# Another element order for the first chunk of activations in a linear-attention plus feed-forward kernel

## The chip, the cores and the metric

The kernel runs on one core of a Trainium2 chip. Its engines are TensorE (PE: matmuls; PEld: loads of the stationary operand, which overlap PE), VectorE (DVE), ScalarE (ACT), GpSimd (POOL) and SyncE (SP, which here only issues DMAs). Each engine works through its own queue in order; where one needs another's result it waits on a semaphore. The metric is the time of one execution on the device in microseconds, the median of several; lower is better.

## What is computed

Two stages follow each other. The first is a linear attention over 8 batches of 8 heads, 576 tokens and 64 dimensions; the second is a feed-forward layer over the 4608 tokens of 512 features.

```
q_s = exp(q - max(q, -1));  q_s = q_s / (sum(q_s, -1) + 1e-9)      # over the head's 64 dimensions
k_s = exp(k - max(k, 2));   k_s = k_s / (sum(k_s, 2) + 1e-9)       # over the 576 tokens
kv  = einsum('bhsd,bhse->bhde', k_s, v)
x   = einsum('bhsd,bhde->bhse', q_s, kv)  as [4608, 512]           # tokens x (heads * 64)
h   = x @ w_in                                                      # [4608, 2048]
g   = h * 1 / (1 + exp(-beta * h))
out = g @ w_out                                                     # [4608, 512]
```

All inputs and the output are f32 in DRAM; the large matmuls run in bf16.

## The kernel before

**Chunks and units.** The feed-forward layer works on x transposed: features on the 128 partitions, in four k tiles (kt 0 to 3), 512 tokens along the free axis. A *chunk* is 512 tokens. Chunks 0 to 6 are the first 512 tokens of the batches 0 to 6, chunk 7 holds the last 64 tokens of all eight batches, chunk 8 is batch 7. A *unit* is one chunk with 128 of the 2048 hidden features, so there are 16 units for each chunk, numbered through: 0 to 15 are chunk 0. A unit n goes through three steps, named in the plan `h_n`, `th_n`, `g_n` and `o_n`: four matmuls, one for each k tile, add up x times w_in in a PSUM bank (`st1`, line 863, matmul at 879); ACT takes the tanh (line 897) and DVE gates with it (line 914); four matmuls multiply by w_out into the accumulators (line 945).

**The order.** A plan written out by hand (`ORDER`) lists all steps, and each engine's queue gets its instructions in this order. `uses` and `made` in the code only check that the plan does not run ahead of itself. The waits between engines are put in by the framework that builds the program, from what each instruction reads and writes of a tile.

**Chunk 0.** PE has nothing to do for the feed-forward layer until x of batch 0 is there; until then it runs filler matmuls (line 367, on a constant or on the exponentials `eqe`) between the attention's own. So that it can begin early, chunk 0 is cut in two halves of 256 tokens, h = 0 and 1 (`cols(h)`), for the units 0 to 3. Two such units share a PSUM bank for each half. In the plan `h_n_h_x` stands for unit n, half h and the k tiles x and x + 2; whole units are `h_n`.

**x of batch 0.** x leaves PE in four PSUM banks, one for each half h and each member jp of a pair of heads (`x_mm`, line 688, written `x_0_h_J`). A bank holds, for both J = 0 and 1, 256 tokens of k tile 2J + jp. Four evacuations, `xev_0_h_jp` in the plan, cast them from f32 to bf16 into the tile `xT[0]` (`x_ev_half`, line 714; it calls `cast`, whose instruction has line 232 on ACT and 234 on DVE). `xT[0]` is laid out as [k tile, 512 tokens], so one evacuation writes two pieces of 256 elements: one in k tile jp and one in k tile 2 + jp. Within a piece the tokens are written in an order with a step of two elements.

The part of the plan around it:

```
xev_0_0_0=dve, qrcp_0_2, x_0_1_1, qnorm_0_2_0=pool,
qnorm_0_2_1=pool, xev_0_0_1=act, x_0_1_0, fill_10, fill_5, cast_w2_0=pool, ld_w2_1, xev_0_1_0=dve, ld_w1_0, ld_w1_1,
cast_w2_1=pool, h_0_0_0, h_0_0_1, h_1_0_0, h_1_0_1, h_0_1_0, xev_0_1_1=act, th_0_0, th_1_0, h_0_1_1, qmax_1_2,
h_1_1_0, h_1_1_1, ld_w4_0, g_0_0, ld_w4_1, qmax_1_3, h_2_0_0, h_2_1_0, ld_k1_0, th_0_1, th_1_1, g_0_1, qsub_1_1=pool,
```

Behind these come the halves of the units 2 and 3, then `h_6`, `h_4`, `h_5`, `h_7` as whole units and `o_0_1`, the first step with w_out. The weights are loaded in f32 and cast to bf16 in blocks: `cast_w0` (first block of w_in, units 0 to 3), `cast_w2` (second block of w_in, units 4 to 7), `cast_w1` and `cast_w3` (first and second block of w_out).

**Later use of the tile.** `xT` has two buffers; `xT[0]` is written again for chunk 2 (`x_ev`, line 707), which like all other chunks writes one k tile of 512 tokens at a time, in the layout [k tile, 512 tokens].

Of the kernel before, what the change touches and what calls it, by code (L numbers as in the profile page):

```python
# [117 lines left out]
def kernel(  # L118
# [40 lines left out]
    def sbt(name, shape, dt):  # L159
        return sb.tile(shape, dt, name=name)  # L160
# [30 lines left out]
    xT = [sbt(f"xT{i}", [P, KT, 512], BF16) for i in range(2)]  # L191
# [14 lines left out]
    def take(*who):  # L206
        assert sum(last in done for last, _ in turns) >= len(who), who
        for w in who:
            n = next(n for n, (last, _) in enumerate(turns) if last in done)
            i = turns.pop(n)[1]  # L210
            place[w] = ring[i][:]
            turns.append((w, i))

    def made(what, *parts):
        done.update((what, p) for p in parts)

    def uses(what, *parts):
        for p in parts:
            assert (what, p) in done, (what, p)
# [10 lines left out]
    def cast(eng, dst, src):  # L230
        if eng is act:
            act.copy(dst, src)  # L232
        else:
            eng.tensor_copy(dst, src)  # L234
# [57 lines left out]
    for b in range(B):  # L292
        n = 2 if b else 1
# [26 lines left out]
    def cast_w(n, half, eng, c0=0, c1=512):  # L320
        which, blk = W[n]
        s = wst[n % 4][:, 2 * half : 2 * half + 2, c0:c1]
        if which == "i":
            made("i", *[(4 * blk + c // P, half) for c in range(c0, c1, P)])
            cast(eng, w_in_b[:, 2 * half : 2 * half + 2, 512 * blk + c0 : 512 * blk + c1], s)
        else:
            made("o", 2 * blk + half)
            cast(eng, w_out_b[:, 4 * blk + 2 * half : 4 * blk + 2 * half + 2, :], s)

    for n in range(8):  # L330
        for half in range(2):
            op(f"ld w{n} {half}", lambda n=n, half=half: load_w(n, half))
            if n == 0:
                for c, (c0, c1) in enumerate(((0, P), (P, 512))):
                    op(
                        f"cast w{n} {half} {c}",
                        lambda e, n=n, half=half, c0=c0, c1=c1: cast_w(n, half, e, c0, c1),
# [361 lines left out]
    def mixed(x):  # L699
        return x.rearrange("p (t c i) -> p t i c", i=2, c=64)  # L700
# [6 lines left out]
    def x_ev(b, j, eng):  # L707
# [3 lines left out]
        done.add(("x", b, j))  # L711
        cast(eng, mixed(xT[b % 2][:, j, :]), place[("x", b, j)].rearrange("p (t i c) -> p t i c", i=2, c=64))

    def x_ev_half(b, jp, h, eng):
        uses("xmm", (b, 0, h), (b, 1, h))
        made("xT", (b, jp, h), (b, 2 + jp, h))
        x = xT[b % 2][:].rearrange("p (J c) (t n i) -> p c J t i n", c=2, i=2, n=64)
        w = place[("x", b, jp, h)].rearrange("p (J t i n) -> p J t i n", J=2, t=2, i=2)
        cast(eng, x[:, jp, :, 2 * h : 2 * h + 2], w)

    def xt_mm(b):
        uses("kvn", *pairs_of(b, 0, 2))
# [55 lines left out]
    for h in range(3):  # L778
        i0, i1 = 4 * h, min(4 * h + 4, NI)
        for J in range(2):  # L780
            p = dict(j=2 * J, n=2, i0=i0, i1=i1)
            op(f"qmax 0 {h} {J}", lambda p=p: q_max(0, **p))
            if (h, J) in QPE:
                op(f"qin 0 {h} {J}", lambda h=h, J=J: q_in(h, J))
                op(f"qminus 0 {h} {J}", lambda h=h, J=J: q_minus(h, J))
            else:
                op(f"qsub 0 {h} {J}", lambda e, p=p: q_sub(0, eng=e, **p), "pool")
            op(f"qexp 0 {h} {J}", lambda p=p: q_exp(0, **p))
            op(f"qsum 0 {h} {J}", lambda p=p: q_sum(0, **p))
            if h < 2:  # L790
                op(f"qrcp 0 {h} {J}", lambda p=p: q_rcp(0, **p))
            op(f"qnorm 0 {h} {J}", lambda e, J=J, i0=i0, i1=i1: q_norm(0, 2 * J, 2, e, i0, i1), "pool")
            if h < 2:
                op(f"qtr 0 {h} {J}", lambda J=J, h=h: q_tr(0, J, 4 * h, 4))
                op(f"qtrev 0 {h} {J}", lambda e, J=J, h=h: q_tr_ev(0, J, 4 * h, 4, e), "act")
                op(f"x 0 {h} {J}", lambda J=J, h=h: x_mm(0, J, h))
                op(f"xev 0 {h} {J}", lambda e, J=J, h=h: x_ev_half(0, J, h, e), "dve" if J else "act")
            else:
                op(f"qtrtev 0 {J}", lambda e, J=J: q_tr_ev(0, J, NM, 1, e), "act")
        if h == 2:  # L800
            op(f"qrcp 0 {h}", lambda i0=i0, i1=i1: q_rcp(0, 0, KT, i0, i1))
# [37 lines left out]
    def chunk_x(c):  # L839
        if c == TAILS:  # L840
            return xTt
        return xT[(c if c < TAILS else c - 1) % 2]

    def halves(h):
        return (0, 1) if h is None else (h,)

    def cols(h):
        return slice(0, 512) if h is None else slice(256 * h, 256 * h + 256)
# [3 lines left out]
    def bank(n, h):  # L852
        key = ("h", n) if h is None else ("hp", n // 2, h)
        if key not in place:
            take(key)
        if h is None:
            return place[key]
        return place[key][:, 256 * (n % 2) : 256 * (n % 2) + 256]
# [4 lines left out]
    def st1(n, ks=(0, 1, 2, 3), h=None):  # L863
        c, u = divmod(n, NJ)
        x = chunk_x(c)
        for kt in ks:
            uses("i", (u, kt // 2))
            if c == TAILS:
                uses("xTt", *[(b, kt % 2) for b in range(B)])
            else:  # L870
                uses("xT", *[(c - (c > TAILS), kt, a) for a in halves(h)])
        if h is not None and n % 2 and ks[0] == 0:
            uses("st1", (n - 1, h))
        if ks[0]:
            uses("begun", (n, h))
        made("begun", (n, h))
        w = bank(n, h)
        for kt in ks:
            pe.matmul(  # L879
                w,  # L880
                w_in_b[:, kt, u * P : (u + 1) * P],
                x[:, kt, cols(h)],
                start=(kt == 0),
                stop=(kt == KT - 1),
            )
        if KT - 1 in ks:
            made("st1", *[(n, a) for a in halves(h)])
# [93 lines left out]
    for n in range(NU):  # L981
        if n < LEAD:
            for h in range(2):
                for x in range(2):
                    op(f"h {n} {h} {x}", lambda n=n, h=h, x=x: st1(n, (x, x + 2), h))
                op(f"th {n} {h}", lambda n=n, h=h: tanh(n, h))
                if n % 2 == 0:
                    op(f"g {n} {h}", lambda n=n, h=h: gate(n, h))
                op(f"o {n} {h}", lambda n=n, h=h: st2(n, h))
            continue  # L990
        if n in (16, 17):
            op(f"h {n} 0", lambda n=n: st1(n, (0, 1)))
            op(f"h {n} 1", lambda n=n: st1(n, (2, 3)))
        else:
            op(f"h {n}", lambda n=n: st1(n))
        op(f"th {n}", lambda n=n: tanh(n))
        op(f"g {n}", lambda n=n: gate(n))
        if n >= NU - LAST:
            for t in range(3):
                op(f"o {n} {t}", lambda n=n, t=t: st2(n, ts=[t]))  # L1000
            for x in range(2):
                op(f"o {n} 3 {x}", lambda n=n, x=x: st2(n, ts=[3], xs=[x]))
        else:
            op(f"o {n}", lambda n=n: st2(n))
# [12 lines left out]
    with tc.manual_schedule():  # L1017
        for name, _, e in plan:
            fn, eng = ops[name]
            eng = e or eng  # L1020
# [31 lines left out]
```

## Time and profile before

| | |
|---|---|
| median of 3 runs | 288.67 us (288.48 to 288.77) |
| the profiled execution | 288.57 us |
| its span, first to last instruction | 286.8 us |
| granted TensorE clock over the span | 0.999 |
| PE, share of the span busy | 96% |
| DVE | 68% |
| ACT | 61% |
| POOL | 46% |

Times in the rows are microseconds from the start of the span, unless they are called ns. A row in order of time begins with the start and the length of one or several merged instructions, then engine, line, operation, what it writes and reads, and their number; in brackets stands for how long the engine was idle before it, and what ended that. `xT<-acc` are the evacuations of batch 0, `xT<-hT` those of the later batches, since these go through the banks called hT. Matmuls are pipelined: the length of one is longer than the distance to the next.

### The profile page before, as it was taken

To read this page: it belongs to the slowest core of one execution; us is meant where nothing else is said; L and a number is where in the kernel's file an instruction comes from. 1 tells how busy PE (TensorE), PEld (TensorE's weight loads), DVE (VectorE), ACT (ScalarE), POOL (GpSimd) and SP (SyncE) were. 2 spreads that over 40 slices of the span, in tenths; PEclk is the share of its full clock that TensorE was granted. 3 is DMA by queue.
4 is the path that set the end of the run, shared out by engine and by line. 5 is a ranking of instruction groups with operands and counts; after the bars stand their busy time and mean duration, and the time that the engine had idled before them with its cause. 6 is when DMAs were issued, how large, how long until landed. Compare 5 with 4: busy or idle time off the path is not lost.

```text
span 286.8 us, 5158 instructions
## 1 busy us (share of the span) xinstructions
PE 276.6 (96%) x1947; PEld 130.0 (45%) x1977; DVE 194.7 (68%) x393; ACT 174.3 (61%) x291; POOL 131.2 (46%) x93
## 2 busy tenths in 40 slices
PE   7798999999999999999999999999999999999994
PEld 3355544444444544444444444444444444444442
DVE  2996966999899898987667948555754254435420
ACT  2488885887498567846587556564672274345422
POOL 6897896959469958082970561090020000000000
PEclk9999999999999999999999999999999999999999
DMA  7999999990891994991533907000054001004204
GB/s 225 396 388 387 384 390 391 369 346 4 225 385 50 292 278 192 299 325 61 165 119 98 235 29 192 0 3 2 0 123 181 0 0 39 0 0 180 78 1 146
DMA packets 36905, 50.01 MB, mean 174 GB/s; under 512 B 15745, under 2 KB 16017, under 8 KB 36881
## 3 DMA queue, kind: packets, MB, share of 16 engines
q1 hardware_dynamic: 36736, 49.56, 52.9%
q8 instruction: 15, 0.25, 0.3%
q10 hardware_dynamic: 144, 0.13, 0.1%
q14 instruction: 10, 0.07, 0.1%
HBM read 36.71 MB, written 9.44 MB: 161 GB/s over the span
## 4 chain that ended last, share of the span: by engine, by line
PE 91%; DVE 3%; DMA 2%; ACT 2%; issue 1%; SPq 0%; DVEq 0%
PE hT L879 43%; PE acc L945 42%; DMA qf<-in_q_dram 2%; PE hT L638 2%; PE hT L688 1%; DVE km L490 1%; DVE qs L428 1%; PE hT L937 1%; PE acc L937 1%; DVE qm L378 1%; ACT ek L612 0%; SPq L275 0%; ACT w_in_b L232 0%; PE hT L464 0%; DVE xT L234 0%
## 5 line engine op out<-in xcount | busy, mean ns | idle before, releaser
L897 ACT ACTIVATE th<-hT,beta_c 128x512 bf16<-128x512 f32 (+1 forms) x148 | 96.6, 676 | 66.7 <-PE hT L879 47.3
L914 DVE SCALAR_TENSOR_TENSOR g<-th,hT 128x512 bf16<-128x512 bf16 x144 | 94.7, 680 | 60.4 <-ACT th L897 57.2
L945 PE MATMUL acc<-w_out_b,g 128*128 128x512 bf16 x543 | 130.7, 380 | 1.4 <-issue 0.8
L879 PE MATMUL hT<-xT,w_in_b 128*128 128x512 bf16 (+1 forms) x517 | 118.0, 373 | 1.9 <-ACT xT L232 0.8
L879 PEld LDWEIGHTS <-w_in_b 128*128 128x128 bf16 x592 | 57.5, 98 | 66.5 <-issue 1.0
L945 PEld LDWEIGHTS <-g 128*128 128x128 bf16 x560 | 53.7, 98 | 64.5 <-issue 2.9
L560 POOL TENSOR_TENSOR kf<-kf,kmb 128x1152 f32<-128x1152 f32 (+1 forms) x15 | 38.0, 2546 | 23.6 <-DVE kmb L550 17.7
L441 POOL TENSOR_TENSOR qn<-eqe,qz 128x1152 bf16<-128x1152 bf16 (+2 forms) x20 | 34.5, 1738 | 28.1 <-DVE qz L433 18.1
L393 POOL TENSOR_TENSOR qf<-qf,qm 128x1152 f32<-128x1152 f32 (+2 forms) x20 | 34.4, 1734 | 19.4 <-issue 14.5
L378 DVE TENSOR_REDUCE qm<-qf 128x9 f32<-128x576 f32 (+2 forms) x34 | 23.3, 703 | 5.9 <-DMA qf<-in_q_dram 5.9
L422 ACT ACTIVATE eqe<-qf 128x576 bf16<-128x576 f32 (+2 forms) x34 | 21.5, 657 | 9.3 <-POOL qf L393 9.3
L232 ACT CAST xT<-hT 128x512 bf16<-128x512 f32 x19 | 12.5, 739 | 21.1 <-PE hT L688 21.1
L428 DVE TENSOR_REDUCE qs<-eqe 128x9 f32<-128x585 bf16 (+2 forms) x34 | 24.0, 713 | 0.5 <-ACT eqe L422 0.4
L490 DVE TRANSPOSE_TENSOR_REDUCE km<-kf 128x18 f32<-128x576 f32 x32 | 23.6, 754 | 0.0
L612 ACT ACTIVATE ek<-kf 128x576 bf16<-128x576 f32 x30 | 19.5, 682 | 0.9 <-POOL kf L560 0.9
L234 POOL CAST va<-vf 128x1152 bf16<-128x1152 f32 (+1 forms) x11 | 12.0, 1104 | 7.0 <-DMA vf<-in_v_dram 7.0
L879 PE MATMUL hT<-xTt,w_in_b 128*128 128x512 bf16 x63 | 14.9, 380 | 0.1
L234 DVE CAST xT<-hT 128x512 bf16<-128x512 f32 x9 | 6.3, 727 | 7.0 <-PE hT L688 7.0
L232 ACT COPY osb<-acc 128x512 f32<-128x512 f32 x14 | 7.8, 594 | 3.0 <-PE acc L945 3.0
L367 PE MATMUL hT<-g,warm 128*128 128x512 bf16 x21 | 7.7, 520 | 1.6 <-POOL g L240 1.5
L234 DVE COPY osb<-acc 128x512 f32<-128x512 f32 (+1 forms) x6 | 3.8, 632 | 4.9 <-PE acc L937 3.8
L638 PEld LDWEIGHTS <-ek 64*64 64x64 bf16 x576 | 5.7, 106 | 2.2 <-issue 1.3
(73 smaller groups left out, 121.8 us busy)
## 6 DMA issues: line engine op xcount, KB each, us to landing
qf<-in_q_dram SPq DMA_DIRECT2D x14, 576.0 KB, 6.2
kf<-in_k_dram SPq DMA_DIRECT2D x14, 576.0 KB, 7.9
vf<-in_v_dram SPq DMA_DIRECT2D x14, 576.0 KB, 7.3
out_dram<-osb SPq DMA_DIRECT2D x19, 256.0 KB, 2.6
wst<-in_moe_w_in_dram SPq DMA_DIRECT2D x8, 512.0 KB, 8.3
wst<-in_moe_w_out_dram SPq DMA_DIRECT2D x8, 512.0 KB, 10.2
out_dram<-wst SPq DMA_DIRECT2D x16, 256.0 KB, 3.7
qf<-in_q_dram SPq DMA_DIRECT2D x4, 288.0 KB, 4.0
```

Source lines behind the costliest of these rows:

```text
L234: eng.tensor_copy(dst, src)
L378: dve.tensor_reduce(qm[:, j : j + n, i0:i1], qf[b % 2][:, j : j + n, i0:i1], axis=AX.X, op=ALU.max,)
L393: eng.tensor_tensor(x, x, m, ALU.subtract)
L422: act.activation(eq[:, i0:i1, j : j + n, :].rearrange("p i j d -> p j i d"), x, ACTF.Exp)
L428: dve.tensor_reduce(qs[:, i0:i1, j : j + n].unsqueeze(3), x, axis=AX.X, op=ALU.add)
L441: eng.tensor_tensor(qn[b % 2][:, i0:i1, j : j + n, :], eq[:, i0:i1, j : j + n, :], z, ALU.mult)
L490: dve.tensor_reduce(km[:, j : j + n].rearrange("p j i e -> p (j i e)"), kf[b % 2][:, j : j + n].rearrange("p j i (e c) -> p (j i e) c", c=32),
L560: eng.tensor_tensor(x, x, m, ALU.subtract)
L879: pe.matmul(w, w_in_b[:, kt, u * P : (u + 1) * P], x[:, kt, cols(h)], start=(kt == 0), stop=(kt == KT - 1),)
L897: act.activation(th[turn(n, h) % 3][:, c], bank(n, h), ACTF.Tanh, scale=beta_c[:, u : u + 1])
L914: dve.scalar_tensor_tensor(out=out, in0=of, scalar=1.0, in1=src, op0=ALU.add, op1=ALU.mult)
L945: pe.matmul(acc[t][:], g[n % NG][:, t * P : (t + 1) * P], w_out_b[:, u, :], start=(u == 0), stop=(u == NJ - 1),)
```

## The change

`xT[0]` gets a second view, `x_first`, which orders its 2048 elements as [half h, member j, J, 256 tokens] instead of [k tile, 512 tokens]. The evacuations of batch 0 write through this view, and all units of chunk 0 read through it. An evacuation thus writes 512 adjacent elements. A half unit reads 256 adjacent elements for each k tile, as before but elsewhere in the tile. A whole unit (4 to 15) reads two pieces of 256 elements, 1024 elements apart, where it read 512 adjacent ones; its PSUM bank is written through a view of two halves, which are adjacent. The plan is not touched, and the later chunks keep the old layout, also in `xT[0]`.

```diff
+    x_first = xT[0][:].rearrange("p k t -> p (k t)").rearrange("p (h j J c) -> p j J h c", h=2, j=2, J=2)
+
     def x_ev_half(b, jp, h, eng):
         uses("xmm", (b, 0, h), (b, 1, h))
         made("xT", (b, jp, h), (b, 2 + jp, h))
-        x = xT[b % 2][:].rearrange("p (J c) (t n i) -> p c J t i n", c=2, i=2, n=64)
+        x = x_first[:, jp, :, h].rearrange("p J (t n i) -> p J t i n", i=2, n=64)
         w = place[("x", b, jp, h)].rearrange("p (J t i n) -> p J t i n", J=2, t=2, i=2)
-        cast(eng, x[:, jp, :, 2 * h : 2 * h + 2], w)
+        cast(eng, x, w)
...
         w = bank(n, h)
+        if c == 0 and h is None:
+            w = w.rearrange("p (h c) -> p h c", h=2)
         for kt in ks:
+            r = x[:, kt, cols(h)]
+            if c == 0:
+                r = x_first[:, kt % 2, kt // 2]
+                r = r if h is None else r[:, h]
             pe.matmul(
                 w,
                 w_in_b[:, kt, u * P : (u + 1) * P],
-                x[:, kt, cols(h)],
+                r,
                 start=(kt == 0),
                 stop=(kt == KT - 1),
             )
```

## The prediction

> **What bounds the kernel now.** I read the page first, then the waits of the stretch from 19 to 23 us, then the order of time from 8 to 31 us, and last the stage sums up to 66 us.
>
> ```profile
> span 286.8 us, 5158 instructions
> PE 276.6 (96%) x1947; PEld 130.0 (45%) x1977; DVE 194.7 (68%) x393; ACT 174.3 (61%) x291; POOL 131.2 (46%) x93
> PE 91%; DVE 3%; DMA 2%; ACT 2%; issue 1%; SPq 0%; DVEq 0%
> 22.90:66.00 43.10, 42.77 (x293) 21.10 (x297) 36.19 (x74) 34.67 (x59) 33.98 (x23) 1.00 0.99 365
> 66.00:276.00 210.00, 208.22 (x1458) 96.18 (x1481) 140.94 (x278) 123.83 (x203) 78.34 (x38) 1.00 0.41 121
> ```
>
> TensorE is the bound: 96% busy, 91% of the chain that ended last. In the two stage rows the first number after the length is PE's busy time: from 22.9 us on it idles for 0.33 us of 43.10 and for 1.78 us of 210. So PE's time can only be won ahead of 22.9 us, where first the attention of batch 0 must be done, and there the change lies. These are all the waits above 0.3 us of that place (who waited for whom, us in total, times, longest):
>
> ```profile
> ACT xT L232 <- PE hT L879: 1.7, 1, 1.7
> PE hT L879 <- ACT xT L232: 0.8, 1, 0.8
> PE hT L879 <- DVE xT L234: 0.4, 1, 0.4
> ```
>
> And the same in order of time (start, length, engine, line, operation):
>
> ```profile
> 19.43 0.41 PE L688 MATMUL acc<-qT,kvn 64*64 64x256 bf16 x8
> 19.48 0.74 DVE L234 CAST xT<-acc 128x512 bf16<-128x512 f32 x1 [0.22 <-ACT beta_c L349]
> 19.62 0.77 ACT L232 CAST xT<-acc 128x512 bf16<-128x512 f32 x1
> 20.18 0.70 DVE L234 CAST xT<-acc 128x512 bf16<-128x512 f32 x1
> 20.27 0.27 PE L879 MATMUL hT<-xT,w_in_b 128*128 128x256 bf16 x1
> 20.94 1.16 PE L879 MATMUL hT<-xT,w_in_b 128*128 128x256 bf16 x9 [0.40 <-DVE xT L234]
> ...
> 22.14 0.73 ACT L232 CAST xT<-acc 128x512 bf16<-128x512 f32 x1 [1.75 <-PE hT L879]
> 22.73 0.83 ACT L897 ACTIVATE th<-hT,beta_c 128x256 bf16<-128x256 f32 x2
> 22.91 6.02 PE L879 MATMUL hT<-xT,w_in_b 128*128 128x256 bf16 x38 [0.81 <-ACT xT L232]
> ```
>
> The four CASTs are the evacuations xev_0_h_J, in the order (half 0, member 0) on DVE, (0, 1) on ACT, (1, 0) on DVE, (1, 1) on ACT. The first ten matmuls are h_0_0_0, h_0_0_1, h_1_0_0, h_1_0_1, h_0_1_0. Two waits are odd. The second matmul reads kt 2 of half 0, written by the first evacuation like kt 0, which began at 20.27; yet it starts at 20.94, after the third evacuation (20.18 + 0.70 = 20.88), which writes half 1. And the last evacuation, whose input was ready at 19.43 + 0.41 = 19.84 and whose engine was free at 20.39, waits 1.75 us until the tenth matmul has read its data, though nothing before it reads what it writes.
>
> One reading explains both. In xT[0] (k tile times 512 + token) an evacuation writes two pieces of 256, 1024 apart; as one interval from its first to its last element, (0,0) covers 0 to 1280, (0,1) 512 to 1792, (1,0) 256 to 1536 and (1,1) 768 to 2048. The second matmul reads 1024 to 1280, inside (1,0); the first reads 0 to 256, outside it. The fifth pair, h_0_1_0, reads 1280 to 1536 with its second matmul, inside (1,1), and that is the one the ACT cast waits for. So the waits are those of interval against interval. Two evacuations whose intervals meet ran at once (19.48 and 19.62), so two-piece write against two-piece write is told apart; only a single-piece read against a two-piece write is not.
>
> **The change part by part.** In the new order of xT[0] (half, member, J, 256 tokens) evacuation (h, j) writes 512 adjacent elements from h*1024 + j*512, and the reads of the units 0 to 3 are single pieces of 256 inside them. No instruction is added, removed or put elsewhere in any queue, no DMA is touched, no wait is added.
>
> *The evacuations themselves.* Same 512 elements, same inner order and same step of two elements. Those of batch 1, which already write one piece each, give the price:
>
> ```profile
> L232 ACT CAST xT<-hT 128x512 bf16<-128x512 f32 x19 | 12.5, 739 | 21.1 <-PE hT L688 21.1
> L234 DVE CAST xT<-hT 128x512 bf16<-128x512 f32 x9 | 6.3, 727 | 7.0 <-PE hT L688 7.0
> ```
>
> 739 and 727 ns stand against 0.70 to 0.77 us above: I take no difference, bounds -0.04 to +0.04 us for the one that could matter.
>
> *The false wait of the second matmul.* Nine matmuls take 1.16 us with one length of 0.27 us in it, so they are issued every (1.16 - 0.27) / 8 = 0.111 us. Without the wait the second starts at 20.27 + 0.11 = 20.38. The third reads what ACT ends at 19.62 + 0.77 = 20.39 and has its turn at 20.49, 0.1 us later: no wait. The ninth (half 1, member 0) has its turn at 20.27 + 8 x 0.111 = 21.16, and DVE ends at 20.88: none either.
>
> *The false wait of the last evacuation.* ACT starts it when it is free, at about 20.43, and ends at 20.43 + 0.74 = 21.17. The eleventh matmul, which now starts at 22.91, has its turn at 20.27 + 10 x 0.111 = 21.38: 0.2 us to spare, and this is the next thing that would be late. Gain of PE here: 22.91 - 21.38 = **1.53 us**. At the least the two idle times go, 0.40 + 0.81 = 1.21; the rest is the length of matmuls that had to end, not only be issued, before ACT could go.
>
> *Does it stay won?* The 38 matmuls from 22.91 run without a break, so what feeds them must come 1.53 us sooner. tanh of the first pair waits for matmul eight: 20.27 + 7 x 0.111 + 0.27 = 21.32 instead of 22.73, 1.41 sooner. What hangs on it:
>
> ```profile
> 21.46 2.02 POOL L234 CAST w_in_b<-wst 128x1024 bf16<-128x1024 f32 x2
> ...
> 23.59 0.69 DVE L914 SCALAR_TENSOR_TENSOR g<-th,hT 128x512 bf16<-128x512 bf16 x1 [2.08 <-ACT th L897]
> 24.20 0.75 DVE L378 TENSOR_REDUCE qm<-qf 128x9 f32<-128x576 f32 x1
> ...
> 25.03 2.12 POOL L393 TENSOR_TENSOR qf<-qf,qm 128x1152 f32<-128x1152 f32 x1 [1.55 <-DVE qm L378]
> ```
>
> DVE waited 2.08 us for that tanh, POOL 1.55 us for the DVE reduction behind the gate; so DVE and POOL move 1.4 us with it, and the later tanhs, which wait for PE, the full 1.53. The first whole unit, h_6, comes after 22 half matmuls: 22.91 + 22 x 0.111 = 25.35 now, 23.82 then. Its weights are POOL's two casts, done at 21.46 + 2.02 = 23.48 and not moved: 0.3 us to spare. Its bank is freed by the gate at 23.59 + 0.69 - 1.4 = 22.9.
>
> What cannot come sooner is the data from DRAM, for the DMA share up to 66 us is 0.99. The load with the least time between landing and use that I found is the second half of w_out's second block:
>
> ```profile
> L318 SPq DMA_DIRECT2D wst<-in_moe_w_out_dram x1: 688/688/688, 25.5 to 25.5; - x1
> DMA to landing us min/median/max: 11.1/11.1/11.1
> 38.56 1.06 ACT L232 CAST w_out_b<-wst 128x1024 bf16<-128x1024 f32 x1
> ```
>
> It lands at 25.5 + 11.1 = 36.6 and is cast at 38.56: 1.96 us, above 1.53. So I let the whole gain stand until the end.
>
> *The whole units 4 to 15 of chunk 0* (12 x 4 = 48 matmuls) read two pieces of 256, 1024 apart. No matmul of the trace has just that; the nearest are the fillers that read eqe in pieces of 64 (two at a time), beside those that read one piece:
>
> ```profile
> 7.81 0.81 PE L367 MATMUL hT<-g,warm 128*128 128x512 bf16 x3
> 9.82 0.38 PE L367 MATMUL hT<-g,warm 128*128 128x512 bf16 x1
> 10.47 1.02 PE L580 MATMUL acc<-kf,ident_f 128*128 128x512 f32 x2
> 13.38 0.59 PE L367 MATMUL hT<-eqe,warm 128*128 128x512 bf16 x2
> ```
>
> One piece: (0.81 - 0.38) / 2 = 0.215 us each. Eight pieces: 0.59 - 0.38 = 0.21. So two pieces cost nothing; as the rows are rounded to 0.01 us, the bounds are -0.005 to +0.005 us each, 48 of them -0.25 to +0.25 us. The costliest 512 columns of the trace are the f32 ones, 1.02 / 2 = 0.51 us each; that end is 48 x (0.51 - 0.215) = 14 us, and I keep it for a rival.
>
> By the Trainium skill (Advanced Engine Details and Errata, SBUF Cachelines) accesses that stay in a 16-byte line run at full performance; 256 bf16 values fill 32 such lines, so by it too these reads would cost nothing, as the fillers' rows say.
>
> *The sum.* The profiled execution took 288.57 us, 1.77 us of it outside the span of 286.8. 288.57 - 1.53 = 287.04. The median of the runs is 0.10 above that execution, so **287.1 us**.
>
> **The rivals.** *Half of it.* If only ACT's false wait goes, the tenth matmul starts at 20.94 + 8 x 0.111 = 21.83 as now and the eleventh at 21.94: gain 0.97, 287.7. If only the matmul's goes, ACT waits until 20.27 + 9 x 0.111 + 0.27 = 21.54, ends about 22.3 and PE resumes at about 22.35: gain 0.56, 288.1. For it: one of the two waits may have another cause. Against: one reading fits both, to the matmul. A part of the gain lost at one of the spare times above (0.2, 0.3, 0.4 us) ends in the same region. Chance 0.12.
>
> *The change does not do what it says*: the waits stay, as the written element order still has a step of two. Against it speaks chunk 1, whose evacuations write one piece with that step:
>
> ```profile
> 49.30 1.93 ACT L232 CAST xT<-hT 128x512 bf16<-128x512 f32 x3 [3.12 <-PE hT L688]
> 50.25 3.62 PE L879 MATMUL hT<-xT,w_in_b 128*128 128x512 bf16 x16
> ```
>
> PE reads the finished k tiles from 50.25 while ACT writes the others until 51.23. Time 288.7. Chance 0.06.
>
> *The other side: the split read is slow.* Each of the 48 matmuls would pay for its second piece, PE having nothing to hide it behind. It cancels the gain at 1.53 / 48 = 0.032 us each; to lose 0.2% takes 0.044. At the rate of the f32 row, +14 us, it would be 301. Against it stand the eqe fillers. The Trainium skill (Advanced Engine Details and Errata, PSUM Cachelines) says that any non-contiguous access pattern "significantly slows down matmuls"; here the output is only viewed as two halves and stays adjacent in its bank, so by its words the rule would not bite, and no run here shows it. Chance 0.06.
>
> **How the numbers follow.** The forecast has 0.76. I call 0.2%, 0.58 us, what a measurement of this kernel can tell from no change. The forecast's own range is 287.1 with +-0.25 for the reads and 0.1 for evacuations and run-to-run, 286.75 to 287.45; the range reaches to 288.1 to take in the halved gains and to 286.7 below; the unchanged and the slow-read case are left out. Faster: 0.76 and nearly all of the 0.12, 0.86. The same: 0.06 and a little of both neighbours, 0.08. Slower: 0.06.
>
> **What would show it.** In the changed profile the first ten matmuls of the unit line stand in one row with the rest, from about 20.3 us, with no idle time put down to a cast; the fourth evacuation starts near 20.4 on ACT; PE resumes the eleventh matmul near 21.4; its tanh starts near 21.3 and the unbroken run that now ends at 22.91 + 6.02 = 28.93 ends near 27.4. The matmuls of the whole units of chunk 0 still follow each other every 0.215 us. Wrong it would be if PE shows new idle time between 22 and 66 us, at h_6 or behind a landing, that eats the 1.5 us, or if those matmuls come more slowly.

## The result and the profile after

The changed kernel takes 287.09 us (median of 6 runs, 286.42 to 287.56) against 288.72 us of the kernel before (6 runs beside it, 288.21 to 289.06). The ratio is 0.9945, with a 95% interval of 0.9929 to 0.9962: faster by 0.4 to 0.7%. Six more runs, called e11 below, gave 287.16 us and 0.9956 (0.9942 to 0.9969). The prediction was 287.1.

First the page of the changed kernel (span, busy time by engine, shares of the chain that ended last), then its two long stages, where the first number after the length is PE's busy time.

```profile
span 285.3 us, 5190 instructions
PE 278.8 (98%) x1977; PEld 130.2 (46%) x1977; DVE 194.6 (68%) x393; ACT 174.3 (61%) x291; POOL 131.2 (46%) x93
PE 92%; DMA 4%; ACT 1%; SPq 1%; issue 0%
```

```profile
22.90:66.00 43.10, 43.10 (x293) 20.50 (x291) 36.78 (x76) 34.87 (x58) 35.53 (x23) 1.00 0.99 365
66.00:276.00 210.00, 210.00 (x1483) 96.21 (x1482) 140.39 (x277) 123.63 (x203) 76.87 (x38) 1.00 0.42 121
```

The span is 1.5 us shorter; the other engines do the same work in the same time, and the DMA share of the first stage is still 0.99. The chain's DMA share, 4% against 2%, lies ahead of 16.3 us, in the first loads. PE is now shown without a pause from 22.9 to 276 us. Against the kernel before, that is only bookkeeping: the trace of before has 1947 matmul records and this one 1977, and a lost record can look like idle time. Here is the same run of matmuls with w_out, before and after; before it lacks its first record:

```profile
47.21 1.67 PE L945 MATMUL acc<-w_out_b,g 128*128 128x512 bf16 x7 [0.16 <-issue]
```

```profile
45.52 1.90 PE L955 MATMUL acc<-w_out_b,g 128*128 128x512 bf16 x8
```

From the first matmul with w_out to the last row of PE's matmuls both kernels take the same time, 282.52 - 28.77 = 253.75 us before and 281.06 - 27.30 = 253.76 us after. So the 0.33 and 1.78 us of idle time read from the two rows of before were such losses, and nothing was won there.

The place of the change, in order of time (start, length, engine, line, operation; line 889 is what was 879, 907 the tanh, 924 the gate, 955 the matmul with w_out; in the experiments the line of the first of these is 879, 880, 889 or 896):

```profile
19.56 0.75 DVE L234 CAST xT<-acc 128x512 bf16<-128x512 f32 x1 [0.21 <-ACT beta_c L349]
19.70 1.37 ACT L232 CAST xT<-acc 128x512 bf16<-128x512 f32 x2
...
20.27 0.72 DVE L234 CAST xT<-acc 128x512 bf16<-128x512 f32 x1
20.36 7.11 PE L889 MATMUL hT<-xT,w_in_b 128*128 128x256 bf16 x48
...
21.49 1.65 ACT L907 ACTIVATE th<-hT,beta_c 128x256 bf16<-128x256 f32 x4 [0.42 <-PE hT L889]
21.55 2.02 POOL L234 CAST w_in_b<-wst 128x1024 bf16<-128x1024 f32 x2
22.36 0.69 DVE L924 SCALAR_TENSOR_TENSOR g<-th,hT 128x512 bf16<-128x512 bf16 x1 [0.74 <-ACT th L907]
...
23.79 2.12 POOL L393 TENSOR_TENSOR qf<-qf,qm 128x1152 f32<-128x1152 f32 x1 [0.23 <-DVE qm L378]
...
27.30 1.89 PE L955 MATMUL acc<-w_out_b,g 128*128 128x512 bf16 x8
```

Both ACT evacuations are merged in one row: the second follows the first at once, where it had waited 1.75 us. All 48 matmuls stand in one row, where there had been three with two pauses: the 32 of the half units (256 columns) and, merged with them, the 16 of the whole units 6, 4, 5 and 7 (512 columns). The first matmul with w_out starts at 27.30 instead of 28.77. This execution began its first evacuation 0.08 us later than the one of before (19.56 against 19.48), so from there 1.55 us are won.

What could have taken the gain back was data that lands at its own time. The load with the least spare time in the prediction lands at 25.5 + 11.2 = 36.7 us, as before, and is cast at 37.10: of 1.96 us of spare time 0.4 are left. (First the issue and its time to landing, then the cast in order of time.)

```profile
L318 SPq DMA_DIRECT2D wst<-in_moe_w_out_dram x1: 732/732/732, 25.5 to 25.5; - x1
DMA to landing us min/median/max: 11.2/11.2/11.2
```

```profile
37.10 1.06 ACT L232 CAST w_out_b<-wst 128x1024 bf16<-128x1024 f32 x1
```

### The profile page after: what moved, and what is told of

The parts are those of the page before. It is cut to its first block, busy times and chain, and to the rows that moved or that the text cites. A ratio compares the mean times of both kernels' runs of the same rounds, so it can differ in the third digit from the quotient of the medians.

```text
span 285.3 us, 5190 instructions
## 1 busy us (share of the span) xinstructions
PE 278.8 (98%) x1977; PEld 130.2 (46%) x1977; DVE 194.6 (68%) x393; ACT 174.3 (61%) x291; POOL 131.2 (46%) x93
## 4 chain that ended last, share of the span: by engine, by line
PE 92%; DMA 4%; ACT 1%; SPq 1%; issue 0%
PE hT L889 44%; PE acc L955 43%; DMA kf<-in_k_dram 2%; DMA wst<-in_moe_w_in_dram 2%; PE hT L638 2%; PE hT L688 1%; SPq L275 1%; PE hT L947 1%; PE acc L947 1%; ACT w_in_b L232 0%; PE hT L464 0%; PE hT L734 0%; ACT qT L232 0%; ACT ek L612 0%; PE hT L367 0%
## 5 line engine op out<-in xcount | busy, mean ns | idle before, releaser
L955 PE MATMUL acc<-w_out_b,g 128*128 128x512 bf16 x560 | 133.0, 379 | 0.0
L367 PEld LDWEIGHTS <-warm 128*128 128x128 bf16 x30 | 3.6, 124 | 7.1 <-issue 5.3
```

The source lines that it names most:

```text
L955: pe.matmul(acc[t][:], g[n % NG][:, t * P : (t + 1) * P], w_out_b[:, u, :], start=(u == 0), stop=(u == NJ - 1),)
```

## The experiments

The start of the first evacuation differs between executions (18.91 to 20.00 us, see the end), so that spans can't be compared directly. Beside the times I use the stretch from the start of the first evacuation to the end of the span: 286.8 - 19.48 = 267.3 us before, 285.3 - 19.56 = 265.7 us after.

**The waits without the layout (e1).** The layout of before, with two small evacuations for each large one:

```diff
-        cast(eng, x[:, jp, :, 2 * h : 2 * h + 2], w)
+        for J in range(2):
+            cast(eng, x[:, jp, J, 2 * h : 2 * h + 2], w[:, J])
```

> Layout and reads of before; each evacuation of batch 0 is two CASTs of 256 columns, each writing one piece. Theory (single-piece reads wait by intervals for two-piece writes): both waits go, as in the changed kernel. ACT's four small casts take longer than two large ones (the 128x256 weight casts took 0.42 to 0.44 us, two of them 0.86 against 0.74), so the eleventh matmul, whose turn is near 21.4, waits up to 0.2 us: 1.3 to 1.55 us won, 287.1 to 287.4. Rival (the gain comes from where the data lies or how PE reads it, not from waits): no gain, 288.7.

Measured: 286.96 us, ratio 0.9944 (0.9932 to 0.9956); stretch 285.3 - 19.53 = 265.8.

```profile
19.67 1.40 ACT L232 CAST xT<-acc 128x256 bf16<-128x256 f32 x4
...
20.27 7.11 PE L880 MATMUL hT<-xT,w_in_b 128*128 128x256 bf16 x48
```

The same 48 matmuls in one row as after the change, with the old layout and the old reads. So neither the place of the data nor the read won the time, but the missing waits. Four casts of 256 columns take 1.40 us and not the 1.7 that I had worked out from the weight casts; nothing is lost.

**Another place (e2).** One string of the changed kernel:

```diff
-... .rearrange("p (h j J c) -> p j J h c", h=2, j=2, J=2)
+... .rearrange("p (j h J c) -> p j J h c", h=2, j=2, J=2)
```

> The changed kernel with the order member, half, J, tokens: every evacuation still writes one piece, at another place, and the two pieces that whole units read are 512 apart instead of 1024. Theory: the same as the changed kernel, 287.1, no wait for a cast between 20.3 and 27 us, matmuls of line 889 still every 0.215 us. Rival (the place or the distance matters): another time by over 0.3 us.

Measured: 286.99 us, 0.9947 (0.9935 to 0.9959); stretch 285.2 - 19.49 = 265.7. As expected: that an evacuation writes one piece decides, not where.

**The first wait alone (e4), the second alone (e5).** The changed kernel with the place of the piece (member j, J, half h) given by a formula; an evacuation writes the pieces `at(jp, 0, h)` and `at(jp, 1, h)`, a whole unit reads `at(j, J, 0)` and `at(j, J, 1)`.

```diff
     # e4: two pieces for member 0, one for member 1
+    at = 1024 * j + (512 * J + 256 * h if j == 0 else 512 * h + 256 * J)
     # e5: one piece for half 0, two for half 1
+    at = 1024 * h + (512 * j + 256 * J if h == 0 else 512 * J + 256 * j)
```

> The changed kernel with member 0 laid out as J, half, tokens and member 1 as half, J, tokens: the evacuations of member 0 write two pieces, those of member 1 one. Theory by intervals: the second matmul reads 512 to 768, inside the interval 256 to 1024 of the third evacuation, and waits for it (starts near 21.0); the fourth evacuation writes one piece that nothing read before touches and starts near 20.4 on ACT; PE then runs without a break. Gain over before 0.97 us, 287.7. Rival (the second wait is a consequence of the first, or has another cause): ACT's fourth evacuation still waits for PE, near 22 us, and nearly all is lost: 288.5 to 288.7.

> The changed kernel with half 1 laid out as J, member, tokens: the evacuations of half 0 write one piece, those of half 1 two. Theory by intervals: the second matmul does not wait; the tenth reads 1536 to 1792, inside the interval 1280 to 2048 of the fourth evacuation, so ACT waits until it has ended, near 21.6, and PE stops for about 0.8 us until near 22.4. Gain over before 0.56 us, 288.1. Rival (the fourth evacuation was late only because the matmuls were): ACT starts it near 20.4 and the time is that of the changed kernel, 287.1.

Measured for e4: 287.32 us, 0.9957 (0.9941 to 0.9973); stretch 285.6 - 19.28 = 266.3, 1.0 us less than before.

```profile
19.43 1.36 ACT L232 CAST xT<-acc 128x512 bf16<-128x512 f32 x2
...
20.07 0.27 PE L896 MATMUL hT<-xT,w_in_b 128*128 128x256 bf16 x1
20.74 7.00 PE L896 MATMUL hT<-xT,w_in_b 128*128 128x256 bf16 x47 [0.40 <-DVE xT L234]
```

Measured for e5: 288.16 us, 0.9985 (0.9973 to 0.9997); stretch 286.7 - 20.00 = 266.7, 0.6 us less than before.

```profile
20.79 1.25 PE L896 MATMUL hT<-xT,w_in_b 128*128 128x256 bf16 x10
22.08 0.73 ACT L232 CAST xT<-acc 128x512 bf16<-128x512 f32 x1 [1.17 <-PE hT L896]
22.86 6.02 PE L896 MATMUL hT<-xT,w_in_b 128*128 128x256 bf16 x38 [0.82 <-ACT xT L232]
```

Each wait can be had alone, each where the intervals put it: in e4 the second matmul waits for the third evacuation and ACT does not, in e5 the ten matmuls run together and ACT then waits for the tenth. The stretches give 1.0 and 0.6 us of gain, where 0.97 and 0.56 were worked out. e4's median is 0.4 us below its forecast; the stretch, which leaves out the differing start, is at it.

**The order alone (e3).** The layout of before; in the plan the fourth evacuation goes ahead of the matmuls:

```diff
-cast_w2_1=pool, h_0_0_0, h_0_0_1, h_1_0_0, h_1_0_1, h_0_1_0, xev_0_1_1=act, th_0_0, ...
+cast_w2_1=pool, xev_0_1_1=act, h_0_0_0, h_0_0_1, h_1_0_0, h_1_0_1, h_0_1_0, th_0_0, ...
```

> Layout of before; in the plan xev_0_1_1 stands ahead of h_0_0_0, so no matmul reads before the fourth evacuation writes. Theory by intervals: nothing is left for ACT to wait for, it starts near 20.4 and ends near 21.15; the second matmul reads inside the interval of that evacuation too and now waits for it, until near 21.2, and PE then runs through: eleventh matmul near 22.2, gain over before 0.7 us, 288.0. Rival (only the order of the plan was at fault, not the layout): 287.1.

Measured: 287.60 us, 0.9953 (0.9935 to 0.9971); stretch 286.5 - 19.45 = 267.05.

```profile
20.24 0.27 PE L879 MATMUL hT<-xT,w_in_b 128*128 128x256 bf16 x1
21.01 7.00 PE L879 MATMUL hT<-xT,w_in_b 128*128 128x256 bf16 x47 [0.50 <-ACT xT L232]
...
166.44 0.63 PE L688 MATMUL hT<-qT,kvn 64*64 64x512 bf16 x8 [0.56 <-DMA qT<-qn]
```

The second matmul now waits for ACT, 0.5 us, as the intervals say. It waits less long than forecast, since ACT ends its second evacuation at 19.59 + 1.36 = 20.95 and not near 21.15. The runs' median is 0.4 us below the forecast, while the profiled execution was the slowest of its runs (288.25): it lost 0.56 us at 166 us, where x of batch 5 waits for the DMA that transposes qn. Without that its stretch is 266.5, 0.8 us less than before. The order of the plan alone gives about half of what the layout gives (1.6 by the same measure); by the rival it would have given all.

**The next thing that is late (e6).** The changed kernel with `xev_0_1_1=dve` in the place of `xev_0_1_1=act`.

> The changed kernel with the fourth evacuation on DVE instead of ACT, behind the third. Theory: the next thing that is late is this evacuation. The third ends near 21.0, the fourth near 21.7, the eleventh matmul, whose turn is near 21.45, waits about 0.25 us; DVE's reduction behind it, 0.7 us later, is still done before the first gate. Time 0.2 to 0.3 us above the changed kernel, 287.35. Rival (there is more to spare than that): no wait, 287.1.

Measured: one time, 287.43 us; stretch 285.6 - 19.48 = 266.1.

```profile
20.18 1.32 DVE L234 CAST xT<-acc 128x512 bf16<-128x512 f32 x2
20.28 7.29 PE L889 MATMUL hT<-xT,w_in_b 128*128 128x256 bf16 x48
...
165.64 0.63 PE L688 MATMUL hT<-qT,kvn 64*64 64x512 bf16 x8 [0.19 <-DMA qT<-qn]
```

The two DVE casts end at 20.18 + 1.32 = 21.50, and the 48 matmuls take 7.29 us instead of 7.11: 0.18 lost here, a little less than the 0.25 expected, and 0.19 of idle time again at the transpose. Together they are the 0.4 us by which the stretch is longer than after; that the time comes near its forecast is partly luck. The fourth evacuation is the next to be late. It ends 21.50 - 20.28 = 1.22 us after the first matmul starts, in the changed kernel (19.70 + 1.37) - 20.36 = 0.71: 0.51 later costs 0.18, so on ACT about 0.3 us are to spare.

**What a split pattern costs PE (e7, e8).** The whole units of chunk 0 in other patterns, the first for what is written, the second for what is read:

```diff
     # e7: the bank is written with a step of two f32
-            w = w.rearrange("p (h c) -> p h c", h=2)
+            w = w.rearrange("p (c h) -> p h c", h=2)
     # e8: x is read with a step of two bf16
-            w = w.rearrange("p (h c) -> p h c", h=2)
+            w = w.rearrange("p (h e c) -> p h e c", h=2, e=2)
-                r = r if h is None else r[:, h]
+                r = r.rearrange("p h (c e) -> p h e c", e=2) if h is None else r[:, h]
```

> The changed kernel, but units 4 to 15 of chunk 0 write their bank with a step of two f32 values, so that their tokens stand in another order and the output of chunk 0 is not the reference's. By the rule that any split access pattern slows matmuls these 48 would come later than every 0.215 us: at double that, 10 us more. Theory of the prediction says nothing of it; the nearest row, the read in eight pieces, says no difference for reads: 287.1 if the write is as free as the read.

> The changed kernel, but units 4 to 15 of chunk 0 read x with a step of two bf16 values inside each half, so that their tokens stand in another order and the output of chunk 0 is not the reference's. If only the number of pieces were free and not the step, the 48 matmuls would come later than every 0.215 us; if PE reads at its pace as long as several values lie in 16 bytes, nothing changes: 287.1. I expect the second.

Measured: 297.11 us for e7 and 286.98 us for e8, one time each. The rows are four whole units of chunk 0 in a row: first of the changed kernel, then of e7, then of e8 (start, length, 16 matmuls).

```profile
36.95 3.61 PE L889 MATMUL hT<-xT,w_in_b 128*128 128x512 bf16 x16
```

```profile
43.56 7.03 PE L889 MATMUL hT<-xT,w_in_b 128*128 128x512 bf16 x16
```

```profile
36.57 3.76 PE L889 MATMUL hT<-xT,w_in_b 128*128 128x512 bf16 x16
```

The kernel before has the same 3.61 us for such 16 (its row starts at 38.41), so reading in two pieces and writing through a view of two adjacent halves costs nothing. A step of two in what is *written* doubles a matmul: the last of the 16 is 0.63 us long there (0.38 in the changed kernel), so one comes every (7.03 - 0.63) / 15 = 0.43 us instead of (3.61 - 0.38) / 15 = 0.215, and 48 of them make the 10 us. By the Trainium skill (Advanced Engine Details and Errata, PSUM Cachelines) any non-contiguous access pattern slows matmuls significantly; for a step in PSUM this trace agrees, 7.03 against 3.61 us. A step of two in what is *read* costs (3.76 - 3.61) / 15 = 0.01 us each. I had expected nothing; 48 of them make 0.5 us, which the stretch shows (285.2 - 18.91 = 266.3, 0.6 more than after) and the time, of an execution that began early, does not. That 0.5 us rests on one execution.

**Is a microsecond of PE here one of the whole? (e9)** Three more filler matmuls ahead of the first unit:

```diff
-... + 8 * [(1, None)]
+... + [(4, None)] + 7 * [(1, None)]
```

> The changed kernel with three more filler matmuls of 512 columns right before the first matmul of the units, 3 x 0.215 = 0.65 us; the first of the unit matmuls now starts near 20.9 instead of 20.36. Theory (a microsecond of PE ahead of the first units is a microsecond of the whole, since landings later leave 1.96 us): about 0.55 us above the changed kernel, 287.65. Rival (something behind has its own time and takes up the difference): under 0.2 us above it.

Measured: 287.59 us, 0.9973 (0.9958 to 0.9988); stretch 285.7 - 19.33 = 266.4.

```profile
19.33 0.75 DVE L234 CAST xT<-acc 128x512 bf16<-128x512 f32 x1 [0.21 <-ACT beta_c L349]
...
20.73 7.11 PE L889 MATMUL hT<-xT,w_in_b 128*128 128x256 bf16 x48
```

In the changed kernel the first matmul comes 20.36 - 19.56 = 0.80 us after the start of the first evacuation, here 1.40: 0.60 us later, and the stretch (266.37 against 265.74) is 0.6 longer. What is lost here is lost at the end.

**A try at more (e10, beside e11, the changed kernel again).** e3 and e6 waited for the transpose of batch 5, whose issue waits for `xt_3` (PE's matmuls for the last 64 tokens of batch 3):

```diff
-g_78, o_69, th_79, g_79, ld_k7_0, th_77, g_77, xt_3, xtev_3_1=act, ...
+g_78, xt_3, o_69, th_79, g_79, ld_k7_0, th_77, g_77, xtev_3_1=act, ...
```

> The changed kernel once more, to stand beside e10 on one chip: 287.0 to 287.1.

> The changed kernel with xt_3 one step with w_out earlier in the plan (ahead of o_69). The transposing DMA of batch 5 waits for xt_3 (its issue went on when that had ended, 157.66 us) and lands 7 to 8 us later, and in the profiled execution of the changed kernel x of batch 5 started 0.16 us after it, in that of e3 after a wait of 0.56. Theory: this landing is the next thing that is late, by 0.2 to 0.6 us in some executions; 0.86 us earlier it is never late, the slowest executions go, and the median is 0.1 to 0.2 us below the changed kernel, 286.9. Rival (the landing follows other DMAs, not its issue): same landing, same time.

Measured: e11 287.16 us, 0.9956 (0.9942 to 0.9969), e10 287.27 us, 0.9957 (0.9940 to 0.9973): no difference. The transpose, its issue in order of time and its time to landing, of e11 (two rows), then of e10 (two rows):

```profile
157.96 4.20 SPq L448 DMA_TRANSPOSE qT<-qn  x1
```

```profile
DMA to landing us min/median/max: 7.5/7.5/7.5
```

```profile
156.95 4.63 SPq L448 DMA_TRANSPOSE qT<-qn  x1
```

```profile
DMA to landing us min/median/max: 8.1/8.1/8.1
```

It was issued 1.0 us earlier and took 0.6 longer, so it landed 0.4 us earlier. The rival was half right, and in 6 runs each nothing is won. In these two executions nothing could be: x of batch 5 starts at 165.54 and 165.55 and waits for the landing in neither. No version beats the changed kernel; e1 and e2 equal it.

## Why the prediction was right, point by point

*The reading of the two waits* as intervals against intervals is shown by e1 (one-piece writes in the old layout take both away), e4 and e5 (each wait alone, at the matmul and the evacuation that the intervals name) and e3 (the fourth evacuation, put ahead of the matmuls, is waited for by the second). The prediction's list of all waits above 0.3 us lacked two of the weight loads (PEld), 1.0 and 0.8 us; they stand before the same two late matmuls and are no third wait. That two two-piece writes are told apart was seen in the trace of before and not tried further.

*The size.* 1.53 us was forecast for the place itself. The first matmul with w_out comes 1.47 us earlier (27.30 against 28.77) in an execution that began 0.08 us later: 1.55 us. The stretch to the end is 1.6 us shorter (267.3 - 265.7), so nothing of it was lost on the way. That 287.09 agrees with 287.1 to 0.01 us is luck: the six runs spread over 1.1 us, and the six of e11 gave 287.16.

*The evacuations* at no difference: 0.75 and 0.72 us on DVE. On ACT two in a row took 1.37 us, where 0.77 + 0.74 = 1.51 had been reckoned; the second only has more to spare by that. *The split reads* at nothing: 3.61 us for 16 matmuls, before and after.

*That it stays won*: the first whole unit had its weights in time, the landings kept their times, and POOL's qsub (line 393) starts at 23.79 instead of 25.03. tanh of the first pair starts at 21.49, where 21.32 plus the 0.08 us of later start was forecast: 0.1 us late, without effect on PE.

*What was mis-read.* The step "from 22.9 us on it idles for 0.33 us of 43.10 and for 1.78 us of 210" took lost records for idle time; PE was busier than that. And the search for data with little spare time ended at 66 us. There is a tighter place behind it. In the changed kernel the transpose of batch 5 lands at 157.72 + 7.4 = 165.1 us, and x of batch 5 starts at 165.28:

```profile
157.72 3.88 SPq L448 DMA_TRANSPOSE qT<-qn  x1
...
165.28 0.63 PE L688 MATMUL hT<-qT,kvn 64*64 64x512 bf16 x8
```

```profile
DMA to landing us min/median/max: 7.4/7.4/7.4
```

e3 and e6 waited there, 0.56 and 0.19 us. But this place does not use up the gain as a load with its own time would: the issue waits for `xt_3` on PE and moves with PE. In the kernel before it was issued at 159.17 us and landed at 166.5, and x of batch 5 started at 166.74, 0.3 us after it; all three came about 1.4 us earlier with the change. What the place adds is scatter, as the time to landing ran from 7.0 us (e9) to 8.2 us (e3).

## What to carry to other kernels

When an engine waits for a result that it does not read, compare the outer bounds of what the two instructions touch. Here a write in two pieces blocked reads between them, and writing one piece, by another order of the buffer or by two smaller instructions, was worth 1.5 us. The wait stood where the bounding engine's dense stretch begins, and nothing behind it made good for it: 0.60 us put in there (e9) were 0.6 us at the end. A split in what a matmul reads was free, a step of two in what it reads cost 0.01 us in 0.215, and a step of two in what it writes doubled its time. Before idle time is believed, the records of the trace are worth counting.

## What had not been expected of the hardware

Executions of the same work differ by when the first loads land; all these kernels do the same up to the first evacuation. The maxima of the first q blocks (line 378) waited 0.80 us for their DMA in e8 and 1.92 us in e5, and the first evacuation began at 18.91 and at 20.00 us; all that lies between moved with it.

```profile
6.76 1.47 DVE L378 TENSOR_REDUCE qm<-qf 128x8 f32<-128x512 f32 x3 [0.80 <-DMA qf<-in_q_dram]
```

```profile
7.85 1.48 DVE L378 TENSOR_REDUCE qm<-qf 128x8 f32<-128x512 f32 x3 [1.92 <-DMA qf<-in_q_dram]
```

That is as large as the effects tested here, and the reason why the stretches from the first evacuation separate the experiments better than single times do.
